# Four numbers in the emission order of a recurrence and feed-forward kernel: unit 1's elementwise part ahead of the last weight conversions, its attention earlier

## The chip, the cores and the metric

The kernel runs on one core of a Trainium2 chip. The metric is the device time of one execution in microseconds (us). Of the kernel before there are three timed runs, 698.75, 700.03 and 700.35 us, with a median of 700.03 us, and one further execution that was profiled.

Four engines matter here. PE multiplies matrices; its weight loads are shown apart as PEld and overlap the matmuls. DVE (VectorE) does the elementwise arithmetic, ACT (ScalarE) the activations, casts and copies, SP (SyncE) only issues transfers. Each engine works off its own list of instructions in order, and semaphores make an instruction wait for others.

## The reference

```
attention (batch 4, 8 heads, 768 steps, head size 48):
    mag   = sqrt(a_re^2 + a_im^2)
    scale = min(mag, 0.999) / (mag + 1e-6)        # a = (a_re, a_im) * scale
    for t in range(768):                          # S is a complex 48 x 48 state per head
        S   = a[t] * S + k[t] (outer) v[t]        # a[t] per row of S, complex
        y[t] = q[t] . real(S)
feed-forward (3072 tokens, 384 -> 1536 -> 384):
    x = y with the heads side by side
    out = ((x @ w_a) * (x @ w_b)) @ w_out
```

All inputs and outputs are 32-bit floats.

## The kernel before, in words

The recurrence is done in chunks of 128 steps. A **unit** is one chunk of two batches, 256 tokens; there are 12 units, 0 to 11. For each unit there are four stages.

- **Elementwise part**, `prep(u)` with `scale` inside it (L166 to L327), on DVE and ACT: it normalises the decays, forms their running products inside the chunk, and multiplies them into q and k in the tile `qk`. It begins with the two multiplications of L210, then a scan of seven pairs L226 and L232, a chain of small steps (L261, L267), the large products of L288 and L293, and ends with two multiplications of L308 that fill `qk`. Between the pairs it also works on the decays of the unit after it (L177 to L192); ACT's steps L179 to L186 belong to that. `prep(1)` does this for unit 1 itself at its head, and for unit 2.
- **Stacking**, `stack(u)` (L332), on the transfer queue of SP: `qk` is copied into the tile `stk`, which the attention reads. It waits for the last L308.
- **Attention**, `attn(u, ...)` (L364), a list of 18 pieces: scores on PE (L378) into a `pm` bank of PSUM, a mask by DVE (L381) into `am`, outputs on PE (L418) into `xp`, transposes (L389) with a copy by ACT (L393), state updates (L441, L448 to L452), and for units 0 and 1 a residual matmul (L430). It ends in `xh` and `xl`, a high and a low part, cast by ACT (L422, L433).
- **Feed-forward**, 12 blocks f = 0 to 11: `gemm1(f)` is 18 matmuls (L485) into an `ab` bank, then ACT, DVE, ACT, DVE (L493 to L496); `gemm2(f)` is 6 matmuls (L503) into `o`, two blocks later.

The weights come as 64-bit numbers and are converted once, block by block, by `split_weights` (L127): for each of three parts of a block, three DVE instructions (L133, L135, L137), a cast by ACT (L141), two matmuls on PE (L146, L147) and a second cast by ACT (L148). Blocks up to 6 use the three `ab` banks, later ones the two `pm` banks, which the attention uses too. The DVE's result `o_sb` has three buffers.

The order of the work has two makers. The Python code at the end of `tile_kernel` hands the stages out in some order: `drain(p1, ns)` takes pieces of `prep(1)` until their stated costs reach `ns`; `next(ws)` hands out one block's conversion; `slot()` hands out pieces of the next unit's attention in the blocks from `ATTN_AT` on. A scheduler then takes that order as priorities and fixes each engine's list before the program runs; `high_priority` moves the feed-forward's and the attention's evictions forward in it. The lists are fixed, so an instruction that waits holds up what is behind it on its engine.

Before, blocks 0 to 5 are converted ahead of unit 0's attention (`CONV_FIRST`), block 6 and on in the feed-forward, `prep(1)` is handed out at 800 per attention piece and 3000 per feed-forward block until block 4 (`P1_AT`), and unit 1's attention from block 5 on.

Of the kernel before, what the change touches and what calls it, by code (L numbers as in the profile page):

```python
# [34 lines left out]
EPS = 1e-6  # L35
A2_MAX = 2.0 ** 60
ST = 8
P1_A = 800
P1_F = 3000
TOK = 2 * C  # L40
RUN = 2 * TOK + 2
# [5 lines left out]
CONV_ON_AB = 7  # L47
NCHK = NU * G + NU + 1
WPART = ((0, DM), (DM, DM), (2 * DM, DM))
CONV_FIRST = 6  # L50
P1_AT = 4
MOE_FIRST = 4000
ATTN_FIRST = 2000
ATTN_AT = (5, 6, 6, 6, 6)
STACK_AT = (11, 11, 11, 10, 10)


# [9 lines left out]
def tile_kernel(ctx: ExitStack, tc: tile.TileContext, a_d, qk_d, v_d, w_d, qn_d, kn_d, vn_d, an_d, out_d):  # L67
# [400 lines left out]
    def pieces(u):  # L468
        return 12 if u % NCH + 1 == NCH else 18
# [142 lines left out]
    def drain(gen, ns=None):  # L612
        if gen is None:
            return
        left = ns
        for cost in gen:
            if left is not None:
                left -= cost or 0
                if left <= 0:
                    return  # L620
# [6 lines left out]
    p1 = prep(1)  # L627
    for _ in range(CONV_FIRST):
        next(ws)
    x_cur = new_x()  # L630
    for _ in attn(0, *x_cur):
        drain(p1, P1_A)
    pend = []
# [12 lines left out]
    for w in range(NU):  # L646
# [5 lines left out]
        os_ = [ps_o.tile([128, 512], F32, name=f"o{t}") for t in range(2)]  # L652
        slots = [0, 2 * (STACK_AT[min(w, 4)] + 1 - max(ATTN_AT[min(w, 4)], 0 if w else P1_AT + 1))]
        left = [pieces(w + 1)]

        def slot():
            if at is None or f < ATTN_AT[min(w, 4)] or (w == 0 and f <= P1_AT) or not slots[1]:
                return
            n = -(-left[0] // slots[1])
            slots[1] -= 1  # L660
            for _ in range(n):
                next(at, None)
                left[0] -= 1

        for f in range(NF):
            if w == 0:
                next(ws, None)
                drain(p1, P1_F)
                if f == P1_AT:
                    drain(p1)  # L670
# [88 lines left out]
```

## Time and profile before

| what | value |
|---|---|
| timed runs, median | 700.03 us (698.75 to 700.35) |
| profiled execution | 700.52 us, of which the profile's span is 698.8 us |
| PE busy, whole span | 654.6 us |
| 0 to 60 us | PE 29.14, DVE 52.25 us busy, mean granted clock of PE 0.74 |
| 60 to 150 us | PE 84.66, DVE 82.28 us busy, clock 0.97 |
| 150 to 699 us | PE 540.82, DVE 415.87 us busy, clock 1.00 |

Times in the profile are microseconds from the start of the span. A row of the timeline has the start, the length, the engine, the line, the operation, output and inputs with shapes, a count, and in brackets the idle time ahead of it with what ended it. A length includes the pipeline's latency, so successive rows of one engine can overlap by some hundredths of a microsecond; what an instruction costs its engine is the distance to the start of the next one. A float matmul is recorded as two instructions where it takes two passes. The clock is the share of TensorE's full clock that was granted.

### The profile page before, as it was taken

Reading aid. Unit: us, or ns where it says so; the run is one execution under the profiler, and the core shown is the slowest. Engines: PE = TensorE matmul, PEld = TensorE weight load, DVE = VectorE, ACT = ScalarE, POOL = GpSimd, SP = SyncE. Lnnn points to the kernel's source line nnn. Section 1 sums busy time; section 2 is a strip of 40 time slices with the busy share of each in tenths; the row PEclk is TensorE's granted clock in tenths of the full one; section 3 lists DMA queues with packets and bytes.
Section 4 is the critical chain, followed back from the end, with each engine's and each line's share of the span. In section 5 each row is a group of like instructions: output and inputs, shape, how many; then the busy total and the mean of one; then the engine's idle time right before and its main releaser. Section 6 shows DMA issues by size and latency. Waiting matters only on the chain.

```text
span 698.8 us, 14287 instructions
## 1 busy us (share of the span) xinstructions
PE 654.6 (94%) x5842; PEld 610.4 (87%) x5842; DVE 550.4 (79%) x1259; ACT 311.4 (45%) x622; POOL 5.6 (1%) x11
## 2 busy tenths in 40 slices
PE   3547999999999999999999999999999999999996
PEld 1224788799899999999999999999999999999996
DVE  6998899998888989989899798999989863233221
ACT  6357656634535446255363564534542332231221
POOL 3000000000000000000000000000000000000000
PEclk9567999999999999999999999999999999999999
DMA  8963300611414205124151340511510500300000
GB/s 312 403 262 93 120 1 0 180 58 58 130 38 130 81 21 157 58 88 132 32 161 45 93 143 2 166 69 47 135 55 2 162 27 17 106 23 2 24 1 27
DMA packets 30231, 63.93 MB, mean 91 GB/s; under 512 B 3664, under 2 KB 7248, under 8 KB 30160
## 3 DMA queue, kind: packets, MB, share of 16 engines
q1 hardware_dynamic: 26704, 58.23, 26.6%
q10 hardware_dynamic: 3456, 4.72, 1.9%
q8 instruction: 48, 0.79, 0.4%
q14 instruction: 23, 0.19, 0.1%
HBM read 39.32 MB, written 4.72 MB: 63 GB/s over the span
## 4 chain that ended last, share of the span: by engine, by line
PE 64%; DVE 26%; DMA 4%; ACT 3%; issue 2%; SPq 1%; DVEq 0%; ACTq 0%
PE ab L485 31%; PE o L503 15%; PE xp L418 6%; PE pm L378 4%; PE pm L441 4%; DVE a_t L288 2%; DMA w<-in_dram 2%; DVE pr L226 2%; DVE qk L308 2%; DVE h_t L494 2%; PE pm L389 2%; DVE hl L496 2%; DMA stk<-qk 1%; DVE am L381 1%; DVE z L232 1%
## 5 line engine op out<-in xcount | busy, mean ns | idle before, releaser
L485 PE MATMUL ab<-xh,w 128*128 128x256 f32 x1728 | 338.7, 285 | 0.0
L485 PEld LDWEIGHTS ab<-xh,w 128*128 128x128 f32 x1728 | 276.6, 189 | 1.9 <-issue 1.4
L485 PE MATMUL ab<-xl,w 128*128 128x256 f32 x864 | 244.6, 283 | 0.0
L485 PEld LDWEIGHTS ab<-xl,w 128*128 128x128 f32 x864 | 162.9, 189 | 0.5 <-ACT xl L433 0.2
L503 PE MATMUL o<-w,hh 128*128 128x384 f32 x576 | 152.4, 345 | 0.0
L493 ACT COPY h_t<-ab 128x256 f32<-128x256 f32 x144 | 53.3, 370 | 184.5 <-PE ab L485 184.1
L494 DVE TENSOR_TENSOR h_t<-ab,h_t 128x256 f32<-128x256 f32 x144 | 60.6, 421 | 70.5 <-ACT h_t L493 69.8
L503 PEld LDWEIGHTS o<-w,hh 128*128 128x128 f32 x576 | 96.8, 188 | 3.7 <-issue 2.8
L503 PE MATMUL o<-w,hl 128*128 128x384 f32 x288 | 97.6, 340 | 0.0
L495 ACT CAST hh<-h_t 128x256 fp32r<-128x256 f32 x144 | 58.0, 403 | 72.6 <-DVE h_t L494 71.4
L496 DVE TENSOR_TENSOR hl<-h_t,hh 128x256 fp32r<-128x256 f32 x144 | 60.6, 421 | 15.6 <-ACT hh L495 15.5
L378 PE MATMUL pm<-stk 128*128 128x128 f32 x384 | 55.3, 282 | 2.6 <-DMA stk<-qk 1.8
L146 PE MATMUL ab<-o_sb,ident 128*128 128x384 f32 x42 | 29.3, 797 | 29.9 <-DVE o_sb L137 29.9
L378 PEld LDWEIGHTS pm<-stk 128*128 128x128 f32 x384 | 49.6, 193 | 7.6 <-issue 4.2
L503 PEld LDWEIGHTS o<-w,hl 128*128 128x128 f32 x288 | 54.0, 188 | 0.1
L226 DVE TENSOR_TENSOR pr<-z 128x384 f32<-128x384 f32 (+1 forms) x91 | 47.2, 525 | 4.3 <-ACT z L212 2.5
L288 DVE TENSOR_TENSOR a_t<-z,b_t 128x768 f32<-128x768 f32 x48 | 45.1, 953 | 0.0
L146 PEld LDWEIGHTS ab<-o_sb,ident 128*128 128x128 f32 x42 | 10.2, 288 | 39.5 <-DVE o_sb L137 29.2
L418 PE MATMUL xp<-am,v_t 128*32 128x128 f32 x768 | 42.5, 277 | 2.1 <-DVE am L381 1.8
L308 DVE TENSOR_TENSOR qk<-qk,z 128x1536 f32<-128x1536 f32 (+1 forms) x26 | 42.3, 1628 | 0.1
L381 DVE TENSOR_TENSOR am<-pm,mask 128x512 f32<-128x512 f32 x48 | 32.8, 686 | 6.7 <-PE pm L378 6.6
L441 PEld LDWEIGHTS pm<-v_t,kt 128*96 128x96 f32 x320 | 32.2, 164 | 1.8 <-issue 1.4
(106 smaller groups left out, 758.7 us busy)
## 6 DMA issues: line engine op xcount, KB each, us to landing
w<-in_dram SPq DMA_DIRECT2D x36, 384.0 KB, 8.1
qk<-in_dram SPq DMA_DIRECT2D x12, 768.0 KB, 4.8
stk<-qk SPq DMA_DIRECT2D x48, 192.0 KB, 3.4
a_t<-in_dram SPq DMA_DIRECT2D x11, 768.0 KB, 4.4
v_t<-in_dram SPq DMA_DIRECT2D x24, 256.0 KB, 2.7
stk<-qk SPq DMA_DIRECT2D x24, 192.8 KB, 3.4
out_dram<-o_sb ACTq DMA_DIRECT2D x24, 192.0 KB, 1.9
stk<-qk SPq DMA_DIRECT2D x16, 128.0 KB, 3.1
```

The costliest lines, as they stand in the source:

```text
L226: vec.tensor_tensor(out=pr[:, :, :, o:o + n], in0=view(zz, W + at_(i) + 2 * o, [[W, 2], [-W, 2], [2, n]]), in1=tok(slice(1, 3), i - 1, o, ...
L288: vec.tensor_tensor(out=pz[:, s].rearrange("p (j b e) -> p j b e", j=SUB // 2, e=2), in0=zb[:, 1 + s], in1=view(bb, (1 + k - s) * NB, [[0, ...
L308: vec.tensor_tensor(out=qk4[:, :, k, x0:x1], in0=qk4[:, :, 1, x0:x1], in1=z[:, k].rearrange("p (j t) -> p j t", j=NJ).unsqueeze(2).broadca ...
L378: pe.matmul(out=sp[:, h4], lhsT=stk[:, h, ks], rhs=stk[:, h, qs], start=True, stop=True)
L418: pe.matmul(out=xp[qd * 32:(qd + 1) * 32, ti], lhsT=l, rhs=rr, start=st, stop=sp_, tile_position=(0, qd * 32), skip_group_check=True)
L441: pe.matmul(out=kp[0:KS, h4 * D:(h4 + 1) * D], lhsT=kts[i, hg][:, h4, :], rhs=v_t[:, o:o + D], start=True, stop=True)
L485: pe.matmul(out=ab[:, m * TOK:(m + 1) * TOK], lhsT=r(w_ab(f, part, m * NJ + i)), rhs=r(xt[:, i, :]), start=n == 0, stop=n == 8)
L493: act.copy(out=h_t, in_=ab[:, 0:TOK])
L494: vec.tensor_tensor(out=h_t, in0=ab[:, TOK:2 * TOK], in1=h_t, op=ALU.mult)
L495: act.copy(out=r(hh), in_=h_t)
L496: vec.tensor_tensor(out=r(hl), in0=h_t, in1=hh, op=ALU.subtract)
L503: pe.matmul(out=os_[tt][:, 0:DM], lhsT=r(ht[:, ts]), rhs=r(w_t[f, 2][:, part, :]), start=(f == 0 and n == 0), stop=(f == NF - 1 and n == 2))
```

## The change

Four constants change; nothing else does.

```
-P1_A = 800
+P1_A = 1500
...
-CONV_FIRST = 6
-P1_AT = 4
+CONV_FIRST = 7
+P1_AT = 0
...
-ATTN_AT = (5, 6, 6, 6, 6)
+ATTN_AT = (3, 6, 6, 6, 6)
```

Seven blocks are converted ahead of unit 0's attention. `prep(1)` is handed out at 1500 per attention piece, and what is left of it in block 0 of unit 0's feed-forward, right behind the conversion of block 7; `stack(1)` follows there. The conversions of blocks 8 to 11 are handed out behind it. Unit 1's attention is handed out from block 3 on (18 turns instead of 14).

What the scheduler makes of it, at three places. Names carry their tile's number.

The first is ACT's list while the last conversions ahead of unit 0's attention are made; `w06` and `w16` are the first two parts of block 6, and L179 and L180 are steps of unit 1's decays. Before:

```order
L177 ACTIVATE a_t_118,chk_104<-a_t_144 128x1536
L141 CAST w25_506<-o_sb_502 128x384
L148 CAST w25_506<-ab_508 128x384
L179 ACTIVATE sc_521<-a_t_118,biases_99 128x768
L180 ACTIVATE sc_521<-sc_521 128x768
L141 CAST w06_755<-o_sb_751 128x384
L181 ACTIVATE sc_521<-sc_521,biases_99 128x768
```

And with the change:

```order
L177 ACTIVATE a_t_118,chk_104<-a_t_144 128x1536
L141 CAST w25_506<-o_sb_502 128x384
L148 CAST w25_506<-ab_508 128x384
L141 CAST w06_516<-o_sb_512 128x384
L148 CAST w06_516<-ab_518 128x384
L141 CAST w16_526<-o_sb_522 128x384
L148 CAST w16_526<-ab_528 128x384
L179 ACTIVATE sc_551<-a_t_118,biases_99 128x768
```

The casts of two parts of block 6 now stand ahead of the decays' logarithm in L179.

The second is PE's list where unit 0's feed-forward ends and unit 1's attention begins (L378 is its first matmul; `ab_1437` and `w011`, `w111`, `w211` belong to block 11, `w210` to block 10). Before, block 11's conversion and its 18 matmuls L485 are already done here:

```order
L485 MATMUL ab_1437<-xh_512,w111_1082 128x256
L503 MATMUL o0_749<-w29_957,hh_1345 128x384 x2
L503 MATMUL o0_749<-w29_957,hl_1346 128x384
L503 MATMUL o1_750<-w29_957,hh_1345 128x384 x2
L378 MATMUL pm_1124<-stk_108 128x128
L503 MATMUL o1_750<-w29_957,hl_1346 128x384
L503 MATMUL o0_749<-w210_1019,hh_1401 128x384 x2
L378 MATMUL pm_1124<-stk_108 128x128
L503 MATMUL o0_749<-w210_1019,hl_1402 128x384
L503 MATMUL o1_750<-w210_1019,hh_1401 128x384 x2
L503 MATMUL o1_750<-w210_1019,hl_1402 128x384
L503 MATMUL o0_749<-w211_1092,hh_1457 128x384 x2
```

And with the change:

```order
L485 MATMUL ab_1437<-xl_543,w011_1054 128x256
L503 MATMUL o0_787<-w29_936,hh_1345 128x384 x2
L503 MATMUL o0_787<-w29_936,hl_1346 128x384
L503 MATMUL o1_788<-w29_936,hh_1345 128x384 x2
L503 MATMUL o1_788<-w29_936,hl_1346 128x384
L503 MATMUL o0_787<-w210_998,hh_1401 128x384 x2
L503 MATMUL o1_788<-w210_998,hh_1401 128x384 x2
L503 MATMUL o0_787<-w210_998,hl_1402 128x384
L503 MATMUL o1_788<-w210_998,hl_1402 128x384
L378 MATMUL pm_1030<-stk_108 128x128 x4
L378 MATMUL pm_1043<-stk_108 128x128
L146 MATMUL pm_1056<-o_sb_1050,ident_91 128x384
```

Only 2 of block 11's 18 matmuls L485 now stand ahead of the first L378. Its three conversions on PE (the first is the last row here), the other 16 and its 6 matmuls L503 follow behind: the conversions and 5 of the 16 among the attention's matmuls, 11 after the attention's last outputs, the 6 behind two blocks of unit 1.

The third is DVE's list from the end of unit 1's elementwise part (the last L308) to the first mask of unit 1's attention (L381); `z_1478` is unit 2's. Before, from the first L210 on:

```order
L210 TENSOR_TENSOR z_1478<-a_t_573,sc_602 128x96x4x2
L496 TENSOR_TENSOR hl_1402<-h_t_1400,hh_1401 128x256
L210 TENSOR_TENSOR z_1478<-a_t_573,sc_602 128x96x4x2
L494 TENSOR_TENSOR h_t_1456<-ab_1437,h_t_1456 128x256
L226 TENSOR_TENSOR pr_1482<-z_1478 128x384
L232 TENSOR_TENSOR z_1478<-pr_1482 128x2x96
L226 TENSOR_TENSOR pr_1485<-z_1478 128x384
L178 SCALAR_TENSOR_TENSOR a_t_573<-a_t_573 128x768
L496 TENSOR_TENSOR hl_1458<-h_t_1456,hh_1457 128x256
L232 TENSOR_TENSOR z_1478<-pr_1485 128x2x96
L226 TENSOR_TENSOR pr_1488<-z_1478 128x384
L381 TENSOR_TENSOR am_1129<-pm_1124,mask_96 128x512
```

And with the change:

```order
L210 TENSOR_TENSOR z_1478<-a_t_580,sc_607 128x96x4x2 x2
L226 TENSOR_TENSOR pr_1482<-z_1478 128x384
L232 TENSOR_TENSOR z_1478<-pr_1482 128x2x96
L226 TENSOR_TENSOR pr_1485<-z_1478 128x384
L232 TENSOR_TENSOR z_1478<-pr_1485 128x2x96
L178 SCALAR_TENSOR_TENSOR a_t_580<-a_t_580 128x768
L226 TENSOR_TENSOR pr_1488<-z_1478 128x384
L232 TENSOR_TENSOR z_1478<-pr_1488 128x2x96
L226 TENSOR_TENSOR pr_1491<-z_1478 128x384
L232 TENSOR_TENSOR z_1478<-pr_1491 128x2x96
L381 TENSOR_TENSOR am_1035<-pm_1030,mask_96 128x512
```

The feed-forward's evictions L494 and L496 are gone from between; two more pairs of the scan stand in their place.

On DVE, from the L308 at 57.75 us of the profile to the last L308 of unit 1, both lists hold the same instructions (55 of the conversions' L133, L135 and L137, all of `prep(1)`, the four masks of unit 0), except that 11 instead of 10 pairs L494 and L496 are in the list of the change. In the units after the second, the lists differ only in how neighbouring instructions interleave.

## The prediction

> **What bounds the kernel now.** I read the page's slices first, then busy time by stage.
>
> ```profile
> PE   3547999999999999999999999999999999999996
> DVE  6998899998888989989899798999989863233221
> 0.00:60.00 60.00, 29.14 (x54) 13.51 (x54) 52.25 (x145) 31.96 (x61) 5.59 (x11) 0.74 0.75 284
> 60.00:150.00 90.00, 84.66 (x701) 72.43 (x702) 82.28 (x191) 55.62 (x111) 0.00 (x0) 0.97 0.29 85
> 150.00:699.00 549.00, 540.82 (x5087) 524.49 (x5087) 415.87 (x927) 223.85 (x451) 0.00 (x0) 1.00 0.24 72
> ```
>
> In the rows by stage the columns are span, then busy time (count) of PE, weight loads, DVE, ACT and POOL, then the clock. From 150 us on PE is busy for 540.82 of 549 us: whatever the change does before, PE carries it unchanged to the end, so the question is when PE has finished unit 0 and unit 1's attention. Up to there DVE is the full engine, and one chain ties the two: DVE's last L308 of unit 1, the stacking, PE's first L378, then the four masks on DVE.
>
> ```profile
> 125.79 1.75 DVE L308 TENSOR_TENSOR qk<-qk,z 128x1536 f32<-128x1536 f32 x1
> 127.46 0.42 DVE L494 TENSOR_TENSOR h_t<-ab,h_t 128x256 f32<-128x256 f32 x1
> 127.79 0.95 DVE L210 TENSOR_TENSOR z<-a_t,sc 128x768 f32<-128x768 f32 x1
> 127.57 7.06 SPq L345 DMA_DIRECT2D stk<-qk  x10
> 130.99 0.49 PE L378 MATMUL pm<-stk 128*128 128x128 f32 x2 [0.46 <-DMA stk<-qk]
> 134.46 0.69 DVE L381 TENSOR_TENSOR am<-pm,mask 128x512 f32<-128x512 f32 x1 [0.36 <-PE pm L378]
> 138.89 0.69 DVE L381 TENSOR_TENSOR am<-pm,mask 128x512 f32<-128x512 f32 x1
> 142.31 0.68 DVE L381 TENSOR_TENSOR am<-pm,mask 128x512 f32<-128x512 f32 x1
> 144.32 0.68 DVE L381 TENSOR_TENSOR am<-pm,mask 128x512 f32<-128x512 f32 x1
> 149.38 0.61 PE L485 MATMUL ab<-xh,w 128*128 128x256 f32 x3
> 150.00 0.39 PE L485 MATMUL ab<-xl,w 128*128 128x256 f32 x1
> ```
>
> L308 leaves DVE at 127.46, the copies are issued at 127.57, PE starts at 130.99, 3.42 us later, after waiting only 0.46 us. So PE's feed-forward of unit 0 and DVE's list end almost together. Attention then runs at the pace of the masks, and unit 1's feed-forward has its `xl` at 150.00.
>
> **The change, part by part.**
>
> *DVE's list up to the last L308.* The change was to bring unit 1's elementwise part forward, but the last L308 still stands behind all conversions: the two lists hold the same instructions, and the new one a pair L494 and L496 more. A pair costs 2 x 0.33 us (127.46 to 127.79 is one), **+0.67 us**. What can differ besides is DVE's waiting in this stretch:
>
> ```profile
> 65.03 0.36 DVE L133 TENSOR_SCALAR o_sb<-w 128x384 uint32<-128x384 uint32 x1 [0.55 <-ACT w L141]
> 66.98 0.69 DVE L381 TENSOR_TENSOR am<-pm,mask 128x512 f32<-128x512 f32 x1 [1.00 <-PE pm L378]
> 78.78 0.56 DVE L226 TENSOR_TENSOR pr<-z 128x384 f32<-128x384 f32 x1 [2.30 <-ACT z L212]
> 83.64 0.36 DVE L133 TENSOR_SCALAR o_sb<-w 128x384 uint32<-128x384 uint32 x1 [0.73 <-PE pm L146]
> 59.61 0.94 ACT L179 ACTIVATE sc<-a_t,biases 128x768 f32<-128x768 f32 x1 [0.21 <-DVE a_t L178]
> 64.89 0.84 ACT L183 ACTIVATE a_t<-sc 128x768 f32<-128x768 f32 x1
> 27.09 0.48 ACT L148 CAST w<-ab 128x384 fp32r<-128x384 f32 x1 [1.51 <-PE ab L147]
> 32.83 0.48 ACT L148 CAST w<-ab 128x384 fp32r<-128x384 f32 x1 [1.02 <-PE ab L147]
> ```
>
> Four waits, 0.55 + 1.00 + 2.30 + 0.73 = 4.58 us. With the change L179 stands behind two conversions on ACT, and L148 of each waits for PE by 1.51 or 1.02 us plus a cast of about 0.5 (these rows are at half clock, as PE is here before too). That puts L179 some 4.5 us later, at about 64, L183 at about 69.5 instead of 64.89, and DVE's L185 behind it. DVE reaches the first mask earlier, since two conversions of block 7 moved ahead, and waits there some 1.5 us; it waits about 1.7 us for L183; then L226's wait falls to about 1.2 us, because ACT's copies of unit 0's attention end when they did and L210 came later. The two waits of L133 go. Together 4.4 us for 4.6; with some small waits of L494 that PE, now with less to do, no longer causes I take **-0.7 us**. Ends: all four waits gone, -4.6; all kept and the new ones added, +3.2. L308 thus ends when it did, 127.5.
>
> *PE ahead of the first L378.* PE has less ahead of it: 16 of block 11's matmuls L485, 3 conversions and 6 matmuls L503 have gone behind.
>
> ```profile
> 667.32 1.06 PE o L503 x6
> 668.38 2.15 PE ab L485 x18
> 82.79 0.81 PE L146 MATMUL pm<-o_sb,ident 128*128 128x384 f32 x2
> 83.61 0.81 PE L146 MATMUL pm<-o_sb,ident 128*128 128x384 f32 x2
> ```
>
> That is 16/18 x 2.15 + 1.06 + 3 x 0.82 = 5.4 us. It doesn't bring the L378 forward, since that waits for `stk` at 131.0 as before; it is idle time instead. The last matmuls ahead need the L496 between the two L308, so PE stops at about 126 and waits some 4.8 us.
>
> *From L308 to the masks.* Without the evictions DVE comes to the first mask by two L210 (1.74), four pairs of L226 and L232 at 0.98 and one L178 (0.87), with about 0.1 us for ACT's L212: 6.6 us against 134.46 - 127.46 = 7.0.
>
> ```profile
> 79.76 0.56 DVE L226 TENSOR_TENSOR pr<-z 128x384 f32<-128x384 f32 x1
> 80.75 0.56 DVE L226 TENSOR_TENSOR pr<-z 128x384 f32<-128x384 f32 x1
> 143.19 0.95 DVE L188 SCALAR_TENSOR_TENSOR a_t<-a_t 128x768 f32<-128x768 f32 x1
> 144.06 0.35 DVE L452 TENSOR_TENSOR u<-u,stk 96x192 f32<-96x192 f32 x1
> ```
>
> But between the second and the third mask there now stand L188, L190 and L192, at 0.87 each (143.19 to 144.06), where L190 and L192 came after the fourth. So by the fourth the lead is gone: 144.2 against 144.32, **-0.1 us**, if PE follows. From 131.6 to the first mask PE can't: the next matmul, a conversion, wants the `pm` bank that the mask frees. That is a second wait of about 3 us.
>
> *Behind the masks.* In the attention's gaps go the three conversions and 5 matmuls. 11 matmuls L485 (11 x 0.12 = 1.3 us) stand between the last outputs and the residual L430, and ACT's L493 of block 11 ahead of the cast L433 of `xl`. Before, PE had small waits there (149.38 to 150.00 holds 0.36 us of work); I set 0.8 us of the 1.3 against these, **+0.5 us**, ends 0 and +1.3. The 6 matmuls L503 of block 11 come after unit 1 has begun, with nothing to hide them: **+1.06 us**.
>
> *The clock.* PE pays for the two waits a second time if the granted clock drops. The trace shows when it does:
>
> ```profile
> 40.12 0.91 PE L146 MATMUL ab<-o_sb,ident 128*128 128x384 f32 x2 [1.13 <-DVE o_sb L137]
> 43.24 1.65 PE L146 MATMUL ab<-o_sb,ident 128*128 128x384 f32 x2 [2.04 <-DVE o_sb L137]
> 42.00:44.00 2.00, 0.76 (x1) 0.50 (x2) 2.00 (x4) 0.51 (x1) 0.00 (x0) 0.54 1.03 398
> 60.00:62.00 2.00, 1.16 (x2) 0.50 (x2) 2.00 (x7) 1.97 (x4) 0.00 (x0) 0.50 0.84 207
> 66.00:68.00 2.00, 1.46 (x10) 1.00 (x8) 1.02 (x2) 1.30 (x3) 0.00 (x0) 0.98 0.53 141
> 138.00:140.00 2.00, 1.13 (x20) 0.73 (x22) 1.91 (x5) 1.22 (x2) 0.00 (x0) 1.00 0.91 309
> ```
>
> One conversion between waits of 1.13 and 2.04 us was too little around 42 us (clock 0.54), while half-busy PE at 138 kept 1.00. From 126 to 134.7 PE would have five L378, some 0.7 us of work; I expect the drop. The clock came back by 66 us, some 5 us after PE got steady work at 60.84. At half clock for 5 us, PE loses up to 2.7 us of work; part lies under DVE's masks. I take the middle, **+1.3 us**, ends 0 and 2.7.
>
> [...]
>
> *Sum* on the profiled execution: 0.67 - 0.7 - 0.1 + 0.5 + 1.06 + 1.3 = +2.7, say **+2.8 us** with some tenths for the `pm` banks that conversions and attention now share. Its span goes from 698.8 to 701.6, with the 1.7 us around it 703.3. That execution (700.52) lies 0.5 us above the median of the runs, so against the median: 700.03 + 2.8 = **702.8 us**.
>
> **Rivals.** *The clock holds and the gaps take block 11.* If PE's two waits fall so that the clock stays at 1.00, and conversions and matmuls fit in the attention's gaps, 0.67 - 0.7 - 0.1 + 0 + 1.06 = +0.9, **700.9 us**. For it: before, PE in attention was half idle. Against it: the row at 42 us. This is also the case in which the change doesn't do what it says, and no more.
>
> *DVE gains.* If ACT's new order removes the waits for L183 and L212 rather than shifting them, all 4.58 us go: L308 ends at 127.46 + 0.67 - 4.6 = 123.5, the stack lands before PE runs out, no clock is lost, and 0.67 - 4.6 - 0.1 + 0.5 + 1.06 gives -2.5, **697.5 us**. It decides where the last L308 ends: below about 125 us the kernel is faster. For it: L226's 2.30 us is the longest wait of the stretch. Against it: L212 stands behind ACT's copies of unit 0's attention in both lists.
>
> *Banks in turn.* The three conversions need a `pm` bank each while masks hold them. If each costs a round trip of 2.03 us (a cast to its second cast at half clock, 25.06 to 27.09) instead of hiding, that is +6 in place of the clock's 1.3: 2.8 - 1.3 + 6 = +7.5, **707.5 us**.
>
> ```profile
> 25.06 0.51 ACT L141 CAST w<-o_sb 128x384 fp32r<-128x384 f32 x1 [1.32 <-DVE o_sb L137]
> ```
>
> **Chances.** A measurement of this kernel can tell about 0.2% from no change, 1.4 us. The forecast 0.50, banks 0.08: both slower, **0.58**. The clock holds 0.25, within 0.2%: **0.25**. DVE gains 0.17: **0.17** faster. The forecast's own range, from the ends of DVE's waits (1.5 us either way the likelier part), tail and clock, is 700.6 to 705.2. The range for the time takes in the second case whole and a part of the third and fourth: **698.8 to 705.6**.
>
> **What would show it.** Right: the last L308 ends between 126 and 129; PE waits over 3 us for `stk`, and again for the first mask; the clock is below 0.8 somewhere from 128 to 140; the fourth mask starts within 1 us of 144.3; unit 1's first `xl` matmul starts after 150 and 6 matmuls L503 of unit 0 follow it. From there on the distance between the two traces stays. Wrong: L308 before 125, or a distance that shrinks after 150, which would mean that PE wasn't the bound there.

## The result, and the profile after

The changed kernel takes **703.75 us** (median of 5 runs, 703.23 to 705.57) against 700.03 before; the ratio is **1.0063, 95% interval 1.0043 to 1.0082**: slower, by 3.7 us on the medians. The profiled execution took 703.23 us with a span of 701.5, so the traces differ by 2.7 us. 702.8 us was predicted.

First the slices of the page of the changed kernel, 17.5 us each (PEclk is the granted clock), and then the clock's row of the kernel before:

```profile
PE   3547999799999999999999999999999999999996
PEclk9976999799999999999999999999999999999999
```

```profile
PEclk9567999999999999999999999999999999999999
```

Before, both rows held a 9 in the eighth digit, 122.5 to 140 us. Now PE is less busy there and its clock is low. The timeline of that place (start, length, engine, line, operation, idle time ahead and its end):

```profile
124.98 1.78 DVE L308 TENSOR_TENSOR qk<-qk,z 128x1536 f32<-128x1536 f32 x1
125.14 0.62 PE L503 MATMUL o<-w,hl 128*128 128x384 f32 x2
130.19 2.20 PE L378 MATMUL pm<-stk 128*128 128x128 f32 x6 [4.43 <-DMA stk<-qk]
132.69 1.34 PE L378 MATMUL pm<-stk 128*128 128x128 f32 x4 [0.30 <-DMA stk<-qk]
133.53 0.69 DVE L381 TENSOR_TENSOR am<-pm,mask 128x512 f32<-128x512 f32 x1
134.27 1.65 PE L146 MATMUL pm<-o_sb,ident 128*128 128x384 f32 x2 [0.24 <-DVE am L381]
140.22 0.69 DVE L381 TENSOR_TENSOR am<-pm,mask 128x512 f32<-128x512 f32 x1 [1.46 <-PE pm L378]
145.29 0.69 DVE L381 TENSOR_TENSOR am<-pm,mask 128x512 f32<-128x512 f32 x1 [0.74 <-PE pm L378]
147.41 0.69 DVE L381 TENSOR_TENSOR am<-pm,mask 128x512 f32<-128x512 f32 x1
154.18 0.28 PE L485 MATMUL ab<-xl,w 128*128 128x256 f32 x1
158.21 0.52 PE L503 MATMUL o<-w,hh 128*128 128x384 f32 x2
```

The last L308 ends at 126.76, 0.8 us earlier than before (127.54). PE stops at 125.76, waits 4.43 us for `stk`, and resumes at 130.19. The masks start at 133.53, 140.22, 145.29 and 147.41, where they started at 134.46, 138.89, 142.31 and 144.32: 0.9 us earlier at the first, 3.1 us later at the fourth. Before, DVE had waited 0.36 us for PE at the first mask and not at the others; now it waits 1.46 and 0.74 at the second and third. Unit 1's `xl` work begins at 154.18 instead of 150.00 (the rows `ab<-xl` ahead of it are block 11's of unit 0), and block 11's L503 follow at 158.21.

The same place in stretches of time (span, then busy time of PE, weight loads, DVE, ACT and POOL, then clock, DMA share and GB/s):

```profile
126.00:128.00 2.00, 0.00 (x0) 0.00 (x0) 1.97 (x3) 0.21 (x1) 0.00 (x0) 1.00 0.05 22
128.00:130.00 2.00, 0.00 (x0) 0.00 (x0) 1.83 (x4) 1.97 (x2) 0.00 (x0) 0.60 0.87 217
130.00:138.00 8.00, 7.27 (x26) 4.74 (x27) 6.70 (x14) 5.01 (x8) 0.00 (x0) 0.50 0.56 147
138.00:140.00 2.00, 2.00 (x15) 1.17 (x14) 0.76 (x2) 0.55 (x2) 0.00 (x0) 0.84 0.97 323
```

A mean of 0.60 over two microseconds of which a part is at 1.00 and the rest at 0.50 puts the drop at 128.4; in the same way 0.84 puts the return at 138.6. **The clock was halved for 10.2 us.** PE "busy" for 7.27 of 8 us is PE at half speed: a pair L146 (the matmul with the identity in a conversion) takes 1.65 us here, 0.81 at full clock.

Later the distance between the traces shrinks. ACT's copies of the outputs (L642), the first of unit 1, the first of unit 3 and the last of all, before:

```profile
207.46 0.48 ACT L642 COPY o_sb<-o 128x384 f32<-128x384 f32 x1
311.04 0.48 ACT L642 COPY o_sb<-o 128x384 f32<-128x384 f32 x1
693.70 0.48 ACT L642 COPY o_sb<-o 128x384 f32<-128x384 f32 x1 [0.47 <-PE o L503]
```

and after:

```profile
212.83 0.86 ACT L642 COPY o_sb<-o 128x384 f32<-128x384 f32 x2
313.81 1.01 ACT L642 COPY o_sb<-o 128x384 f32<-128x384 f32 x2
696.41 0.48 ACT L642 COPY o_sb<-o 128x384 f32<-128x384 f32 x1 [0.47 <-PE o L503]
```

At 158 us PE was 4.2 us behind at the first `xl` matmul and had 1.06 us of L503 to make up, 5.2 us together. At the end of unit 3 the distance is 2.8 us, at the end of the kernel 2.7. Some 2.5 us were regained between 160 and 310 us.

### The profile page after: what moved, and what is told of

The parts are those of the page before. It is cut to its first block, busy times and chain, and to the rows that moved or that the text cites. A ratio compares the mean times of both kernels' runs of the same rounds, so it can differ in the third digit from the quotient of the medians.

```text
span 701.5 us, 14291 instructions
## 1 busy us (share of the span) xinstructions
PE 656.5 (94%) x5842; PEld 611.5 (87%) x5842; DVE 551.7 (79%) x1259; ACT 311.6 (44%) x622; POOL 5.6 (1%) x11
## 4 chain that ended last, share of the span: by engine, by line
PE 71%; DVE 19%; DMA 4%; ACT 3%; issue 1%; SPq 1%; ACTq 0%; DVEq 0%
PE ab L485 35%; PE o L503 16%; PE xp L418 6%; PE pm L378 5%; PE pm L441 4%; DMA w<-in_dram 3%; DVE a_t L288 2%; PE pm L389 2%; DVE qk L308 2%; PE pm L146 2%; DVE h_t L494 2%; DVE z L293 1%; DVE hl L496 1%; DVE pb L261 1%; DVE o_sb L135 1%
## 5 line engine op out<-in xcount | busy, mean ns | idle before, releaser
L485 PE MATMUL ab<-xh,w 128*128 128x256 f32 x1728 | 339.3, 285 | 0.0
L485 PEld LDWEIGHTS ab<-xh,w 128*128 128x128 f32 x1728 | 276.7, 189 | 2.1 <-issue 1.6
L485 PE MATMUL ab<-xl,w 128*128 128x256 f32 x864 | 245.4, 284 | 0.0
L485 PEld LDWEIGHTS ab<-xl,w 128*128 128x128 f32 x864 | 163.0, 189 | 0.7 <-issue 0.2
L503 PE MATMUL o<-w,hh 128*128 128x384 f32 x576 | 152.6, 345 | 0.0
L494 DVE TENSOR_TENSOR h_t<-ab,h_t 128x256 f32<-128x256 f32 x144 | 60.7, 421 | 70.9 <-ACT h_t L493 70.2
L503 PEld LDWEIGHTS o<-w,hh 128*128 128x128 f32 x576 | 97.0, 188 | 3.7 <-issue 2.6
L503 PE MATMUL o<-w,hl 128*128 128x384 f32 x288 | 97.4, 339 | 0.0
L496 DVE TENSOR_TENSOR hl<-h_t,hh 128x256 fp32r<-128x256 f32 x144 | 60.6, 421 | 19.0 <-ACT hh L495 18.6
L378 PE MATMUL pm<-stk 128*128 128x128 f32 x384 | 55.6, 286 | 5.4 <-DMA stk<-qk 5.4
L378 PEld LDWEIGHTS pm<-stk 128*128 128x128 f32 x384 | 50.0, 196 | 9.4 <-DMA stk<-qk 6.0
L146 PE MATMUL ab<-o_sb,ident 128*128 128x384 f32 x42 | 29.1, 794 | 28.5 <-DVE o_sb L137 28.5
L503 PEld LDWEIGHTS o<-w,hl 128*128 128x128 f32 x288 | 54.0, 188 | 0.3 <-DVE hl L496 0.3
L146 PEld LDWEIGHTS ab<-o_sb,ident 128*128 128x128 f32 x42 | 9.8, 276 | 38.8 <-DVE o_sb L137 28.8
L418 PE MATMUL xp<-am,v_t 128*32 128x128 f32 x768 | 40.9, 279 | 2.8 <-DVE am L381 2.5
L308 DVE TENSOR_TENSOR qk<-qk,z 128x1536 f32<-128x1536 f32 (+1 forms) x26 | 42.4, 1630 | 0.2
L381 DVE TENSOR_TENSOR am<-pm,mask 128x512 f32<-128x512 f32 x48 | 32.8, 684 | 5.8 <-PE pm L378 5.3
L418 PE MATMUL xp<-stk,u 128*32 128x128 f32 x640 | 34.6, 274 | 0.0
## 6 DMA issues: line engine op xcount, KB each, us to landing
stk<-qk SPq DMA_DIRECT2D x16, 128.0 KB, 3.1
```

The lines of the kernel that those rows point to most:

```text
L146: pe.matmul(out=lp[:, 0:n], lhsT=ident, rhs=t, start=True, stop=False)
L308: vec.tensor_tensor(out=qk4[:, :, k, x0:x1], in0=qk4[:, :, 1, x0:x1], in1=z[:, k].rearrange("p (j t) -> p j t", j=NJ).unsqueeze(2).broadca ...
L378: pe.matmul(out=sp[:, h4], lhsT=stk[:, h, ks], rhs=stk[:, h, qs], start=True, stop=True)
L418: pe.matmul(out=xp[qd * 32:(qd + 1) * 32, ti], lhsT=l, rhs=rr, start=st, stop=sp_, tile_position=(0, qd * 32), skip_group_check=True)
L485: pe.matmul(out=ab[:, m * TOK:(m + 1) * TOK], lhsT=r(w_ab(f, part, m * NJ + i)), rhs=r(xt[:, i, :]), start=n == 0, stop=n == 8)
L494: vec.tensor_tensor(out=h_t, in0=ab[:, TOK:2 * TOK], in1=h_t, op=ALU.mult)
```

## The experiments

Each was timed together with the kernel before (medians 699.83, 700.10 and 699.98 us in the three groups of runs). Ratios are to that kernel, with the 95% interval; a microsecond is 0.143%.

**1. The attention part undone.** Against the changed kernel:

```
-ATTN_AT = (3, 6, 6, 6, 6)
+ATTN_AT = (5, 6, 6, 6, 6)
```

> The change without its attention part: ATTN_AT begins with 5 as before, the other three numbers stay changed. In this order all of block 11's L485, the conversions and the L503 of block 9 stand ahead of unit 1's first L378 again, as in the kernel before. Theory (the late block 11 leaves PE idle for stk, the clock drops, and PE pays afterwards): the last L308 still ends near 126.7 us, PE's wait for stk ahead of the first L378 is under 1.5 us, the granted clock stays above 0.9 from 126 to 140 us, unit 1's first xl matmul is back at 149 to 150, no L503 of block 11 is left behind it, and the time is that of the kernel before or up to 1 us less: 699.0 to 700.2 us. Rival (the new early order of DVE and ACT costs the time, by its additional waits): the time stays near 703 us.

698.75 us, ratio 0.9995 (0.9981 to 1.0009): no change against before. DVE's L308 and the stacking in its timeline:

```profile
122.67 3.54 DVE L308 TENSOR_TENSOR qk<-qk,z 128x1536 f32<-128x1536 f32 x2
129.67 0.49 PE L378 MATMUL pm<-stk 128*128 128x128 f32 x2 [0.43 <-DMA stk<-qk]
142.59 0.68 DVE L381 TENSOR_TENSOR am<-pm,mask 128x512 f32<-128x512 f32 x1
148.26 0.39 PE L485 MATMUL ab<-xl,w 128*128 128x256 f32 x1
```

L308 ends at 126.21, PE waits 0.43 us, the clock stays at 1.00, `xl` begins at 148.26, a little earlier than expected. So the loss hangs on the one number that hands attention out from block 3, and the new early order costs nothing that can be told (the interval is 1 us either way). (With 4 in its place the engines' lists come out identical to those with 5: the loss begins only where attention is handed out before block 11's conversions and takes the `pm` banks that these want.)

**2. The attention part alone**, on the kernel before:

```
-P1_AT = 4
+P1_AT = 2
-ATTN_AT = (5, 6, 6, 6, 6)
+ATTN_AT = (3, 6, 6, 6, 6)
```

> The kernel before with its attention part given out earlier alone (ATTN_AT begins with 3; P1_AT goes to 2 with it, since the elementwise part has to be given out ahead of the attention; CONV_FIRST and P1_A stay). The conversions of blocks 10 and 11 then stand behind the attention's start in PE's list, one block more than in the change. Theory (block 11 behind the attention costs the time): slower than the kernel before, by at least what the change costs, 3.7 us, up to 7 us: 703.5 to 707 us, with PE waiting over 4 us for stk and the clock at 0.5 somewhere between 125 and 145 us. Rival (it is the early elementwise part that costs): within 1.4 us of 700.0.

707.76 us, ratio 1.0113 (1.0095 to 1.0131), some 8 us slower; a little more than expected. Two blocks are late instead of one, and PE runs dry earlier:

```profile
119.48 0.57 PE L503 MATMUL o<-w,hl 128*128 128x384 f32 x2
127.31 1.58 PE L378 MATMUL pm<-stk 128*128 128x128 f32 x4 [7.25 <-DMA stk<-qk]
```

```profile
120.00:122.00 2.00, 0.05 (x1) 0.00 (x0) 1.97 (x2) 0.00 (x0) 0.00 (x0) 0.85 0.30 83
132.00:134.00 2.00, 2.00 (x12) 0.89 (x12) 1.12 (x4) 0.78 (x3) 0.00 (x0) 0.50 0.32 72
134.00:136.00 2.00, 2.00 (x13) 1.33 (x8) 1.34 (x5) 0.73 (x1) 0.00 (x0) 0.73 0.35 90
```

The wait is 7.25 us, the half clock lasts from 121.4 to 135.1 (worked out from the means as above). Earlier attention is what costs, with either early part.

**3. The wait filled.** The changed kernel with matmuls that nobody reads in place of the idling:

```
+    def filler(n, xh):
+        ab = ps_ab.tile([128, 512], F32, name="ab")
+        for i in range(n):
+            pe.matmul(out=ab[:, 0:TOK], lhsT=r(w_ab(0, 0, i % 6)), rhs=r(xh[:, i % 3, :]),
+                      start=i == 0, stop=i == n - 1)
...
             pend.append((w, f, *gemm1(f, *x_cur), os_))
+            if w == 0 and f == 10:
+                filler(36, x_cur[0])
```

> The changed kernel with 36 matmuls more, 128 x 256 each and read by nobody, which stand right behind the last L485 that PE has ahead of its wait for stk: 36 x 0.119 = 4.3 us of PE work in place of 4.4 us of idling. They compute nothing that is used. Clock theory (half clock for 10 us, 128.8 to 138.7, is what makes masks and PE late): the clock stays above 0.9 from 126 to 140 us, the fourth mask comes 2 to 3 us earlier than 147.4, the first xl matmul is at 151 to 152.5, and the kernel is 1.5 to 3 us faster than the changed one: 700.7 to 702.2 us, although PE has 4.3 us more to do. Rival (the pm banks and DVE's round trips set the pace of this stretch, whatever the clock): fourth mask within 0.5 us of 147.4, time within 0.7 us of 703.7 or above it.

700.51 us, ratio 1.0022 (1.0006 to 1.0038), against 1.0063 (1.0043 to 1.0082) without the filler. The intervals don't meet: PE does 4.3 us more, and the kernel is 0.41%, **2.9 us, faster** (the two intervals together leave 1.1 to 4.6 us). DVE's and ACT's lists are those of the changed kernel; PE's differs by the filler and by two neighbouring L503 that change places. Its timeline and stretches:

```profile
121.15 4.44 PE L648 MATMUL ab<-xh,w 128*128 128x256 f32 x36
124.23 1.74 DVE L308 TENSOR_TENSOR qk<-qk,z 128x1536 f32<-128x1536 f32 x1
129.38 1.01 PE L378 MATMUL pm<-stk 128*128 128x128 f32 x4 [0.39 <-DMA stk<-qk]
144.48 0.69 DVE L381 TENSOR_TENSOR am<-pm,mask 128x512 f32<-128x512 f32 x1
151.25 0.28 PE L485 MATMUL ab<-xl,w 128*128 128x256 f32 x1
```

```profile
130.00:138.00 8.00, 6.45 (x44) 3.96 (x45) 7.41 (x15) 6.09 (x8) 0.00 (x0) 1.00 0.60 147
```

The clock holds, PE does 44 matmul records from 130 to 138 us where it did 26, the fourth mask starts at 144.48 instead of 147.41 and `xl` at 151.25 instead of 154.18, each 2.9 us earlier. Of these, 0.8 us are L308, which ends earlier in this trace though DVE's list is the same. From the end of L308 to the fourth mask the changed kernel takes 20.65 us, this one 18.5 and experiment 1 16.4: the half clock and the late block 11 cost 2.1 us each there. What remains at the end against experiment 1 is the price of the late block 11 at full clock: 0.27% or 1.9 us.

**4, 5, 6. A delay of PE, measured by itself.** The kernel before with unread matmuls at the start of a feed-forward: 45 (5.3 us) in unit 1, 22 (2.6 us) in unit 1, 45 in unit 5.

```
+            if w == 1 and f == 0:
+                filler(45, x_cur[0])
             pend.append((w, f, *gemm1(f, *x_cur), os_))
```

> The kernel before with 45 matmuls more, 128 x 256 each and read by nobody, at the start of unit 1's feed-forward: 45 x 0.119 = 5.3 us of PE work at a place where PE is about full. They compute nothing that is used. It measures what a PE delay at 150 us is worth at the end. Theory from the two traces (5.3 us behind at 150, 2.8 us behind from unit 2 on, since at the stackings of units 2 and 3 PE waited for DVE anyway): the time grows by 2.5 to 3.7 us, 702.5 to 703.7 us, and the distance to the trace of before shrinks between 170 and 230 us. Rival (PE is the bound everywhere from 150 us on, as the prediction had it): the time grows by the whole 5.3 us, to 705.3 us, and the distance stays.

> The kernel before with 22 unread matmuls (22 x 0.119 = 2.6 us of PE) at the start of unit 1's feed-forward, where 45 (5.3 us) cost 2.5 us. It tells what form the regain has. Fixed slack theory (PE has about 3 us of pauses at the stackings of units 2 and 3, which a delay fills first): 22 matmuls cost 0 to 0.4 us, within 0.2% of the kernel before. Rival (a share of every delay is regained, as 2.5 of 5.3): 1.2 us. Second rival (PE the bound, the 45 an odd case): 2.6 us.

> The kernel before with the 45 unread matmuls (5.3 us of PE) at the start of unit 5's feed-forward instead of unit 1's. Theory (the pauses that take up a delay lie at the stackings of units 2 and 3, before 230 us, and PE is the bound later): the whole 5.3 us show, 704.6 to 705.6 us. Rival (DVE or another engine gives way in every unit): 2.5 us again, near 702.5 us.

| delay | time | ratio | cost |
|---|---|---|---|
| 5.3 us in unit 1 | 702.36 us | 1.0033 (1.0022 to 1.0044) | 2.3 us (1.5 to 3.1) |
| 2.6 us in unit 1 | 701.06 us | 1.0008 (0.9998 to 1.0017) | 0.6 us (-0.1 to 1.2) |
| 5.3 us in unit 5 | 706.05 us | 1.0082 (1.0069 to 1.0096) | 5.7 us (4.8 to 6.7) |

The late delay costs all of itself (706.05 us is a little above the range expected), the same delay in unit 1 about half or less. So PE is the bound from unit 5 on and isn't quite in the units before: 3.0 us of 5.3 are taken up there. Of the half delay 2.0 of 2.6 us are taken up; that lies between a fixed slack (0 to 0.4 us cost) and a fixed share (1.2), and the interval reaches to both. The added matmuls also changed how neighbouring instructions of DVE interleave: unit 3's last L308 starts at 215.79 us in the trace of experiment 4, 2.5 us earlier than before, and at 216.14 in that of experiment 5. How much of the small costs comes from this other order of DVE, no run separates.

Where the slack lies shows on DVE and at PE's first L378 of units 2 and 3. Before:

```profile
170.61 1.75 DVE L308 TENSOR_TENSOR qk<-qk,z 128x1536 f32<-128x1536 f32 x1
175.83 0.46 PE L378 MATMUL pm<-stk 128*128 128x128 f32 x2 [0.74 <-DMA stk<-qk]
218.29 1.75 DVE L308 TENSOR_TENSOR qk<-qk,z 128x1536 f32<-128x1536 f32 x1
223.55 0.46 PE L378 MATMUL pm<-stk 128*128 128x128 f32 x2 [0.64 <-DMA stk<-qk]
```

After:

```profile
170.84 1.75 DVE L308 TENSOR_TENSOR qk<-qk,z 128x1536 f32<-128x1536 f32 x1
176.12 0.46 PE L378 MATMUL pm<-stk 128*128 128x128 f32 x2 [0.65 <-DMA stk<-qk]
218.59 1.75 DVE L308 TENSOR_TENSOR qk<-qk,z 128x1536 f32<-128x1536 f32 x1
```

The last L308 of units 2 and 3 start 0.2 and 0.3 us later in the changed kernel, though PE is up to 5 us behind: DVE's elementwise part hardly follows PE, and a PE that is late waits less for it. The wait of 0.64 us at unit 3 is gone, and of the other 0.09. These are only 0.7 of the 2.5 us regained. PE's busy time can hide more; here are the weight loads beside it (before first, then after):

```profile
172.00:192.00 20.00, 19.26 (x206) 17.33 (x206) 17.45 (x35) 10.90 (x18) 0.00 (x0) 1.00 0.43 121
212.00:232.00 20.00, 19.36 (x159) 18.44 (x159) 17.82 (x31) 11.01 (x20) 0.00 (x0) 1.00 0.49 146
```

```profile
172.00:192.00 20.00, 19.35 (x197) 17.84 (x196) 17.86 (x35) 11.31 (x19) 0.00 (x0) 1.00 0.42 122
212.00:232.00 20.00, 19.97 (x153) 19.53 (x152) 19.24 (x34) 12.06 (x23) 0.00 (x0) 1.00 0.48 141
```

PE's busy time in these two stretches grows by 0.7 us, that of the weight loads by 1.6 (35.77 to 37.37). That a matmul which waits for the next counts in the first column and not in the second is a reading of these columns, and the stretches hold different work in the two traces (197 matmuls against 206, 153 against 159). The starts of the matmuls show the pauses more directly. Take the median distance of two neighbouring matmuls of the same lines and shapes over the traces after 160 us, and sum what the single distances have above it. From 212 to 232 us this excess is 2.6 us before, 1.1 in the changed kernel and 0.3 in experiment 4; from 172 to 192 us it is 4.5, 4.0 and 3.5. From 160 to 690 us it is 1.5 us smaller in the changed kernel than before and 2.7 smaller in experiment 4. So PE has pauses around these two stackings that a delay fills. With the waits counted in, they make up most of the 3.0 us that experiment 4 took up; of the 2.5 us that the changed kernel regains, some 1.0 stays open.

**7. No claim on the banks.** The changed kernel with all conversions on `ab` banks:

```
-CONV_ON_AB = 7
+CONV_ON_AB = 12
```

> The changed kernel with CONV_ON_AB = 12: all conversions go through ab banks, so no conversion waits for a pm bank that the attention has claimed. In this order block 11's conversions stand ahead of unit 1's first L378 again, and what fills the attention's gaps is gemm work of blocks 11 and 9 to 11; ahead of the first L378 PE has some 3.6 us less than in the kernel with the attention part undone. Theory, part one (block 11 was late because of the pm banks): no L503 of unit 0 is left after unit 1's feed-forward has begun, 18 L485 of block 11 stand between the first masks. Part two (a wait for stk of 3 us or more halves the clock): PE waits 2.5 to 3.5 us for stk; if the clock drops it does so for up to 10 us, but PE has 4 us of other work between the masks, so the fourth mask comes at 143 to 146 and the time lies between 699 and 702 us, faster than the change. Rival (attention given out early costs what it costs wherever block 11 stands): 703 us or more.

701.38 us, ratio 1.0026 (1.0015 to 1.0037). Part one held: block 11 stands ahead or between the first masks, and none of its L503 come after unit 1 has begun. Of part two the fourth mask (144.38) and the time came as forecast, but not on the way forecast: PE waits 0.79 us for `stk`, not 2.5 to 3.5, and the clock stays at 1.00, so this run doesn't test what such a wait does. (The 3 us were the author's estimate; the traces have drops in waits of 2.04, 4.43 and 7.25 us.)

```profile
130.27 0.46 PE L378 MATMUL pm<-stk 128*128 128x128 f32 x2 [0.79 <-DMA stk<-qk]
144.38 0.69 DVE L381 TENSOR_TENSOR am<-pm,mask 128x512 f32<-128x512 f32 x1
150.13 0.39 PE L485 MATMUL ab<-xl,w 128*128 128x256 f32 x1
```

Masks and `xl` are where they were before the change, so the bank claim is confirmed as what puts block 11 behind the attention. The kernel is still 1.8 us slower than before. PE reaches L378 later than its shorter list says: in this trace it pauses for 0.82, 1.71 and 1.33 us between 91 and 102 us, waiting for `o_sb` and for `hh`, where the trace of the changed kernel has no such pause. The last L308 of unit 2 also starts 0.6 us later than before. What that edit costs without the change was not run, and stays open.

**8 to 11. Later attention in units 2 and 3.** If PE pauses at the stackings of units 2 and 3, attention that is handed out one block later there should gain, with or without the early part:

```
-ATTN_AT = (5, 6, 6, 6, 6)
+ATTN_AT = (5, 7, 7, 6, 6)
```

> The change without its attention part, and the attention of units 2 and 3 given out one block later than in all kernels so far (ATTN_AT = (5, 7, 7, 6, 6)). In this order unit 3's first L378 stands behind more of unit 2's feed-forward, unit 2's first stays where it was and only the end of its attention moves. Theory (PE waits 0.6 to 0.8 us for stk at units 2 and 3): the wait of unit 3's first L378 goes, that of unit 2 stays, 0 to 0.7 us faster than with the attention part undone alone (698.75): 698.0 to 698.8 us. Rival (the attention now ends too late for the next unit's xl, and PE waits there): 700 us or more.

> The kernel before with ATTN_AT = (5, 7, 7, 6, 6) alone: units 2 and 3 give out their attention one block later, the early part stays as before. It tells to which of the two edits the 0.25% of the kernel with both belongs. If the later attention of units 2 and 3 is worth its 0.64 us of waiting at unit 3: 0.3 to 1 us faster than before, 699.1 to 699.8 us. If the new early part carries the gain: no change, 700.0 us. If the gain needs both: in between, and less than 1.7 us.

> The change without its attention part, with ATTN_AT = (5, 7, 7, 6, 6), a second time, beside the kernel with the later attention alone: 698.4 us again, 1 to 2.4 us faster than before.

> The same with ATTN_AT = (5, 7, 7, 7, 7): every later unit one block later too, in eight places instead of ten. From unit 4 on PE waited for nothing at the stackings, so there is no wait to remove: theory 698.4 us or slower, up to +1.5 us, since each unit's attention is pressed into fewer places. A gain of over 1 us against ATTN_AT = (5, 7, 7, 6, 6) would say that PE's waits there are hidden in its busy time.

| kernel | time | ratio |
|---|---|---|
| before, (5, 7, 7, 6, 6) | 698.25 us | 0.9979 (0.9970 to 0.9988) |
| experiment 1, (5, 7, 7, 6, 6) | 698.45 us | 0.9975 (0.9961 to 0.9989) |
| the same again | 697.72 us | 0.9969 (0.9958 to 0.9980) |
| experiment 1, (5, 7, 7, 7, 7) | 701.22 us | 1.0018 (1.0006 to 1.0029) |

One block later for units 2 and 3 gains 1.5 us on the kernel before, more than the 0.64 us of wait that its trace showed and than the 0.3 to 1 us expected. Of that kernel, PE waits for `stk` only once after 150 us:

```profile
174.51 0.46 PE L378 MATMUL pm<-stk 128*128 128x128 f32 x2 [0.83 <-DMA stk<-qk]
```

and in stretches of time:

```profile
212.00:232.00 20.00, 19.98 (x203) 19.52 (x204) 19.65 (x34) 11.60 (x22) 0.00 (x0) 1.00 0.51 143
```

Its weight loads from 212 to 232 us are at 19.52, where the kernel before had 18.44: 1.1 us more, against 0.62 in PE's own column. That agrees with pauses hidden in "busy" but doesn't show them, since the stretch holds other work (203 matmuls against 159). The early part adds nothing that can be told: the intervals of the three faster kernels overlap. All three are faster than both kernels of this case. Later attention in the further units, where no trace showed a wait, loses 0.4 to 0.5% against that. Its trace has PE idle for 2.76 us from 262 to 690 us (428 minus 198.24 and 227.00) instead of 1.50 in the trace of experiment 10; on what, was not followed.

```profile
262.00:462.00 200.00, 198.24 (x1873) 192.19 (x1872) 183.85 (x400) 98.44 (x187) 0.00 (x0) 1.00 0.34 99
462.00:690.00 228.00, 227.00 (x2138) 220.98 (x2137) 132.65 (x301) 72.67 (x161) 0.00 (x0) 1.00 0.16 46
```

## Why the prediction was right, and where it wasn't

The sign, the place and the chain were right, and the sum of +2.8 us met the traces' +2.7. But the sum was met by luck, because two errors nearly cancelled: the loss up to 158 us was priced at 2.8 and was 5.2 (the clock and block 11 among the masks), and the distance was expected to stay and shrank by 2.5. Of the signs that the prediction gave for being right, the fourth mask within 1 us of 144.3 and the staying distance did not come.

*DVE's list.* The last L308 was predicted at 127.5 and ends at 126.76. The waits of that stretch:

```profile
65.87 0.69 DVE L381 TENSOR_TENSOR am<-pm,mask 128x512 f32<-128x512 f32 x1 [0.64 <-PE pm L378]
69.31 0.96 DVE L185 TENSOR_TENSOR a_t<-a_t 128x768 f32<-128x768 f32 x1 [1.30 <-ACT a_t L183]
77.95 0.56 DVE L226 TENSOR_TENSOR pr<-z 128x384 f32<-128x384 f32 x1 [0.65 <-ACT z L212]
```

With 0.40 (L188) and 0.35 (L133) they come to 3.34 us instead of 4.58; 3.9 had been forecast, and the shift from L212 to L183 came as told, somewhat smaller at every place. The rival in which DVE gains enough to bring L308 below 125 fell. The term can't be settled finer: L308 ended between 126.1 and 128.0 in the five traces with the old early lists, between 125.4 and 127.1 in the six with the new ones.

*PE ahead of the first L378.* Right: it stops at 125.76 (126 predicted) and waits 4.43 us (4.8). The second wait, about 3 us for the first mask, did not come: at half clock the ten records of L378 fill the time, and PE waits only 0.30 us for `stk` and 0.24 for the mask.

*The masks, -0.1 us, "if PE follows".* PE didn't follow. The first mask is 0.9 us early, the fourth 3.1 us late.

*The clock, +1.3 us with ends 0 and 2.7.* This is the term that was mis-sized. It was worked out from 5 us at half clock, after the return by 66 us in the trace of before; the clock stayed down for 10.2 us. The filler puts its worth at 2.1 us by the fourth mask and at 2.9 us by the times at the end, within 1.1 to 4.6: above the middle of the forecast, and about at its upper end. In the trace of before the clock returned 5.2 us after PE had resumed (60.84 to 66.06), here 8.4 us after (130.19 to 138.6), with gaps of 0.30 us ahead of 132.69 and 0.24 us ahead of 134.27 in between. What sets that length, no run shows.

*Block 11 behind the masks, +0.5 and +1.06 us.* The tail came as told: the first `xl` matmul after 150, the L503 behind it. With the filler, so at full clock, the late block 11 costs 2.1 us up to the fourth mask against experiment 1, 1.1 more up to the first `xl` (6.77 us after that mask instead of 5.67) and 1.06 in the L503: 4.3 us, of which 1.9 are left at the end. The tail was priced about right; the prediction's sum had nothing for block 11 between the masks, where the conversions now stand, and its rival of the banks in turn had 6 us.

*"From there on the distance between the two traces stays."* Wrong. The prediction read 540.82 of 549 us busy as PE carrying any delay unchanged to the end, and the trace of before held rows against it: two waits of 0.74 and 0.64 us at the stackings of units 2 and 3, and weight loads at 17.33 and 18.44 of 20 us around them. A delay at 150 us is worth 2.3 of its 5.3 us at the end, one at unit 5 all of it. The prediction had named a shrinking distance as the sign that PE wasn't the bound there, and that sign came.

In the ledger of the traces: 0.8 us early at L308, 3.1 late at the fourth mask, 4.2 at the first `xl`, 5.2 with the late L503, 2.5 regained, 2.7 left. The clock-holds rival (+0.9 us) is what experiment 3 comes near to: with the clock held by filler the change costs 0.22%, 1.5 us.

## What to carry to other kernels

Work that is handed out earlier takes buffers earlier, and what is pushed behind may be the other stream's last block; look in the new list for what lost its bank, not only for what moved forward. A PE wait ahead of a latency-bound stage, 4.43 us here, can be paid twice, once as idling and once as half clock through the stage (10.2 us of it here; with 36 matmuls in the wait the clock stayed at 1.00 and the kernel was 2.9 us faster), so keep independent matmuls for that place. And a busy share of 98% (540.82 of 549 us) doesn't mean that a delay comes through to the end: look, stage by stage, for waits and for pauses between PE's matmuls that its busy column doesn't show.

## What the runs showed of the hardware

In the traces of the kernel before and of the changed kernel the granted clock is 1.00 or 0.50 from 40 to 160 us. In the kernel before it falls at 42.17 us, returns at 55.82, falls at 59.23 and returns at 66.06; in the changed kernel it falls at 43.08, returns at 63.56, falls at 128.42 and returns at 138.66. In experiment 2 it is at 0.50 from 121.4 to 135.1 us.

The time from PE's last matmul to the drop was 2.6 us in the changed kernel (125.76 to 128.4), 1.4 in experiment 2 (120.05 to 121.4) and 1.0 before (41.20 to 42.2). The time from PE's resuming to the return was 8.4 us in the changed kernel (130.19 to 138.6), 7.8 in experiment 2 (127.31 to 135.1) and 5.2 before (60.84 to 66.06). So neither is the same from place to place, and no run separates what decides it.

The drops at 128.4 and 121.4 us fell into waits of 4.43 us (the changed kernel) and 7.25 us (experiment 2), those at 42.17 and 59.23 us of the kernel before into waits of 2.04 and 1.95 us; the one at 43.08 us of the changed kernel came 0.1 us after a wait of 2.04 us had ended (at 42.94). Waits of 0.46 us (before), 0.43 (experiment 1) and 0.79 (experiment 7) ahead of unit 1's first L378 went with a clock of 1.00. The clock was also 1.00 in two microseconds of which PE was busy for 1.13 (138 to 140 us in the kernel before), and with the filler in two of which it was busy for 0.85:

```profile
130.00:132.00 2.00, 0.85 (x4) 0.50 (x4) 1.93 (x4) 1.19 (x2) 0.00 (x0) 1.00 0.84 218
```
